# A fused Performer attention and MLP-Mixer kernel: one explicit order list, row-pair projections, and transposes moved to the DMA queue

## The chip, the cores and the metric

The kernel runs on one NeuronCore of a Trainium2 chip. The metric is the device time of one execution in microseconds (us); a case is timed by the median of several executions. The engines named below are TensorE (PE in the profile; PEld is its weight load), VectorE (DVE), ScalarE (ACT), GpSimd (POOL) and SyncE (SP, which here only issues DMAs). POOL issues the DMAs that convert float32 to float16.

## The reference

The inputs are `q`, `k`, `v` of shape (8 batches, 8 heads, 576 rows, 64), a feature matrix `omega` (128, 64), and four mixer weights. What is computed, cut to its core:

```python
def phi(x):                                   # positive random features
    proj = np.einsum('bhsd,md->bhsm', x, omega)
    sq = np.sum(x * x, axis=-1, keepdims=True) / 2.0
    h = proj - sq
    h = h - np.max(h, axis=-1, keepdims=True)
    return np.exp(h) / np.sqrt(m)
q_p, k_p = phi(q * scale), phi(k * scale)     # scale = 64 ** -0.25
kv  = np.einsum('bhsm,bhsd->bhmd', k_p, v)
z   = np.sum(k_p, axis=2)
num = np.einsum('bhsm,bhmd->bhsd', q_p, kv)
den = np.einsum('bhsm,bhm->bhs', q_p, z)[..., None] + 1e-06
x   = (num / den) as (8, 576, 512)

h  = np.maximum(x.transpose(0, 2, 1) @ w_tok1, 0.0) @ w_tok2   # 576 -> 256 -> 576
u  = x + h.transpose(0, 2, 1)
h2 = np.maximum(u @ w_ch1, 0.0) @ w_ch2                        # 512 -> 1536 -> 512
out = u + h2
```

## The kernel before

Each batch's 576 rows are split in 512 "main" rows and 64 "tail" rows. Two rows of 64 values stand side by side on the 128 partitions: partitions 0 to 63 of `qT` and `kT` hold one row of a pair, partitions 64 to 127 the other. For batches 0 and 1 this layout is made with TensorE transposes; for batches 2 to 7 `q` and `k` are first converted to float16 in DRAM (`cast_dram`) and then loaded by a transposing DMA (`load_T`).

The projection multiplies by `bd`, a 128 x 256 matrix that has `omega` transposed in two blocks on its diagonal and zeros elsewhere, so that one 128-deep contraction handles either row of the pair:

```python
def q_proj(b, hp, w):                # called twice per head pair: w = 0, 1
    ...
    ps = att_ps([P, 2, NP2], FP32, "q_ps")
    nc.tensor.matmul(
        ps, bd[:, w * M : (w + 1) * M], sb[:, 2 * hp : 2 * hp + 2, 0:NP2], start=True, stop=True
    )
    exp(live["qp", b, hp][:, w], ...)

def k_proj(b, hp, i):                # called twice per head pair: i = 0, 1
    ...
    ps = att_ps([P, 4, M], FP32, "k_ps")
    for e in range(2):
        nc.tensor.matmul(
            ps[:, 2 * e : 2 * e + 2, :],
            sb[:, 2 * hp + i, e * P : (e + 1) * P],
            bd, start=True, stop=True,
        )
    exp(live["kp", b, hp][:, i], ps)
```

`k_max` takes the maximum of the exponentials per row (two VectorE operations), its reciprocal, and multiplies `v` by it into `v_sc`. For batch 0 that multiplication runs on VectorE, for the others on GpSimd. Then `kv` (eight matmuls of 65 columns and two of 130) gives `kv_ps`, `num` gives `num_ps`, and `norm` divides into `xm`.

The mixer follows: `tok1` and `tok2` over the rows, then for each block of 128 rows a transpose of `u` on TensorE, which the channel layers need:

```python
def u_transpose(src, dst):
    ps = mix_ps([P, ND, P], FP16, "uT_ps")
    for db in range(ND):                                        # 4 transposes
        nc.tensor.transpose(ps[:, db, :], src[:, db * P : (db + 1) * P], ident16)
    nc.vector.tensor_copy(out=dst, in_=ps)

def ch1(c, cb):                      # 12 of these for each of 9 chunks c
    ps = mix_ps([P, SM], FP32, "h3_ps")
    for db in range(ND):             # 4 matmuls of 512 columns
        nc.tensor.matmul(ps, wc1[...], uT[:, db]..., start=(db == 0), stop=(db == ND - 1))
    nc.scalar.activation(out=live["r3", c][:, cb, :], in_=ps, func=AF.Relu)

def ch2(c, j):                       # 4 of these for each chunk
    ps = mix_ps([P, DM], FP32, "h2_ps")
    for cb in range(NCB):            # 12 matmuls of 512 columns
        nc.tensor.matmul(ps, live["r3", c][...], wc2[:, cb, :], ...)
    nc.vector.tensor_tensor(out=o, in0=u, in1=ps, op=ALU.add)
    nc.sync.dma_start(out=out[...], in_=o)
```

Chunk 8 collects the tails of all eight batches. [...]banks: three for `att_ps` (transposes and projections), two for `kn_ps` (`kv`, `num`), three for `mix_ps` (mixer).

[...]In this kernel every step has a place on a common time axis (numbers such as `u + o["kv"]`), and the steps are emitted sorted by place. At its start TensorE runs eight matmuls on zeros (`warm_ps`).

Of the kernel before, what the change touches and what calls it, by code (L numbers as in the profile page):

```python
# [9 lines left out]
FP32 = mybir.dt.float32  # L10
# [7 lines left out]
def kernel(  # L18
# [43 lines left out]
    def att_ps(shape, dt, name):  # L62
        return pspool.tile(shape, dt, name=name, tag="attps", bufs=3)
# [4 lines left out]
    def mix_ps(shape, dt, name):  # L68
        return pspool.tile(shape, dt, name=name, tag="mixps", bufs=3)
# [4 lines left out]
    live = {}  # L74

# [17 lines left out]
    def load_v(b):  # L93

        if b < 2:
            t = ldpool.tile([P, H, NJ, D], FP16, name="v_16", tag="v_16", bufs=2)
            live["v", b] = t
            nc.gpsimd.dma_start(
                out=t.rearrange("p h j d -> p h (j d)"),
                in_=v[b, :, 0:SM, :].rearrange("h (p j) d -> p h (j d)", j=NJ),  # L100
            )
            return
# [8 lines left out]
    def load_v_tail(b):  # L111
        t = ldpool.tile([P, 4, D], FP32, name="v_tail", tag="v_tail", bufs=2)
# [27 lines left out]
    def cast_qk(which):  # L140
        nc.vector.tensor_copy(out=live[which + "nat", 0][:, 0:2, :], in_=stage[which])
# [9 lines left out]
    warm = xt[0]  # L151
    nc.vector.memset(warm, 0.0)
    for b in range(2):
        new_nat(b)
# [5 lines left out]
    make_identity(nc, ident16)  # L160
    load_nat(0, 2, 4, "q")
    load_nat(0, 2, 4, "k")
    load_nat(0, 4, 8, "q")
    load_nat(0, 4, 8, "k")
    load_nat_tail(0, "k")
    load_nat_tail(0, "q")
    load_v(0)
# [5 lines left out]
    omega_nat = wpool.tile([P, 2 * D], FP16, name="omega_nat")  # L173
    nc.vector.tensor_copy(out=omega_nat[:, 0:D], in_=om_f)
    nc.vector.tensor_copy(out=omega_nat[:, D : 2 * D], in_=om_f)

    bd = wpool.tile([P, 2 * M], FP16, name="bd")
    nc.vector.memset(bd, 0.0)
# [11 lines left out]

    om_ps = att_ps([P, P], FP16, "om_ps")
# [3 lines left out]

    nc.vector.memset(w1t, 0.0)

    def clear_vz():
        for t in vz:
            nc.vector.memset(t, 0.0)  # L200

    def clear():
        nc.vector.memset(w2t, 0.0)
        nc.vector.memset(xt[1], 0.0)
        for t in q_pt:
            nc.vector.memset(t[:, 0:ST], 0.0)
            nc.vector.memset(t[:, SM + ST : SM + 2 * ST], 0.0)
# [10 lines left out]
    def permute_w2():  # L218
        for tb in range(NT):
            nc.vector.tensor_copy(  # L220
                out=w2m[:, tb], in_=w2raw[:, tb, 0:SM].rearrange("p (c j) -> p j c", j=NJ)
            )
            nc.vector.tensor_copy(out=w2t[:, tb, 0, 0:ST], in_=w2raw[:, tb, SM:S])
            nc.vector.tensor_copy(out=w2t[:, tb, 1, ST:P], in_=w2raw[:, tb, SM:S])
# [15 lines left out]
    steps = []  # L240

    def at(place, fn, *args):
        steps.append((place, len(steps), fn, args))


    def t_main(b, h0, n, which):

        if h0 == 0:
            live[which + "T", b] = ldpool.tile(
                [P, H, SP2], FP16, name=f"{which}T", tag=f"{which}T", bufs=2  # L250
            )
        ps = att_ps([P, n, 2, P], FP16, "t_ps")
# [5 lines left out]
        copy = nc.vector.tensor_copy if which == "q" else nc.scalar.copy  # L258
        copy(  # L259
# [4 lines left out]
    def t_tail(b, which):  # L264
# [4 lines left out]
        nc.vector.tensor_copy(out=live[which + "T", b][:, :, NP2:SP2], in_=ps)  # L269
# [32 lines left out]
    def k_tail_max(b, eng):  # L302
# [8 lines left out]
        for hh in range(4):  # L311
# [3 lines left out]
            eng.tensor_tensor(  # L315
# [6 lines left out]
    def q_proj(b, hp, w):  # L322
        sb = live["qT", b]
        if w == 0:
            live["qp", b, hp] = apool.tile([P, 2, 2, 2, P], FP16, name="q_p", tag="q_p", bufs=3)
        ps = att_ps([P, 2, NP2], FP32, "q_ps")
        nc.tensor.matmul(  # L327
            ps, bd[:, w * M : (w + 1) * M], sb[:, 2 * hp : 2 * hp + 2, 0:NP2], start=True, stop=True
        )
# [218 lines left out]
    for part in range(2):  # L548
        at(8 + O["kt"] + L["wc2"], load_wc2, part)
# [98 lines left out]
```

The softmax here doesn't subtract the row's maximum and nothing guards it: scores larger than these inputs give would overflow.

## Time and profile before

| what | value |
|---|---|
| time, median of 3 runs | 324.12 us (320.99 to 327.26) |
| span of the profiled execution | 318.9 us |
| VectorE busy | 173.8 us (55%) |
| ScalarE busy | 155.8 us (49%) |
| GpSimd busy | 71.6 us (22%) |
| DMA: packets on the queue of SP, on that of POOL, as a share of 16 engines' span | 32.4%, 26.2% |
| matmuls of `ch1` and `ch2` | 2 x 432, each 128 x 512 |
| projection matmuls | 64 of 128 x 512 (`q`), 128 of 128 x 256 (`k`) |
| TensorE transposes of `u` | 144 of 128 x 128 |

The span is read in slices: a row of 40 digits for each engine, where 9 means a slice of 8 us in which the engine was busy for 90% or more. A duration that the profile gives for a matmul is from its start to its modelled end; consecutive matmuls overlap, so the distance between starts, not the duration, is what one costs when the engine is full.

### The profile page before, as it was taken

The numbers are of one execution on the slowest core, as the hardware profiler recorded it, in microseconds if no ns is written. First come the engines' busy times: TensorE is split into PE (matmuls) and PEld (weight loads), VectorE is DVE, ScalarE is ACT, GpSimd is POOL, SyncE is SP. The second block draws the span as 40 slices with busy tenths as digits, with TensorE's granted clock in tenths as the row PEclk, the third lists the DMA queues.
The fourth block names the chain that finished last, engine by engine and source line by source line (L and its number), as shares of the span: only waits on it lengthen the run. The fifth ranks groups of instructions, "written<-read, shape, count | busy, mean of one in ns | idle before, by whom it ended". The sixth has DMA issues, their size and how long they took to land.

```text
span 318.9 us, 5525 instructions
## 1 busy us (share of the span) xinstructions
PE 299.3 (94%) x2137; PEld 159.1 (50%) x2137; DVE 173.8 (55%) x463; ACT 155.8 (49%) x299; POOL 71.6 (22%) x102
## 2 busy tenths in 40 slices
PE   5657889999999999999999999999999999999993
PEld 1435455555555555555555555555555444444441
DVE  3599996567455745674558456755385244002011
ACT  1557668633673367416842684358523610440610
POOL 9550535402141214121412131112311000000000
PEclk9598999999999999999999999999999999999998
DMA  7999999999990699059905991110011001002014
GB/s 150 195 195 211 192 244 213 196 238 205 153 256 35 128 173 244 25 123 175 259 3 128 158 238 54 68 66 2 1 67 68 0 27 74 33 2 102 30 39 92
DMA packets 59689, 38.75 MB, mean 121 GB/s; under 512 B 31120, under 2 KB 54544, under 8 KB 59280
## 3 DMA queue, kind: packets, MB, share of 16 engines
q1 hardware_dynamic: 48736, 24.16, 32.4%
q0 software_dynamic: 10656, 13.99, 26.2%
q8 instruction: 16, 0.26, 0.3%
q10 hardware_dynamic: 272, 0.26, 0.3%
q14 instruction: 9, 0.07, 0.1%
HBM read 35.88 MB, written 16.52 MB: 164 GB/s over the span
## 4 chain that ended last, share of the span: by engine, by line
PE 81%; DVE 10%; DMA 3%; POOL 3%; issue 1%; ACT 0%; POOLq 0%; DVEq 0%
PE h_ps L507 29%; PE h_ps L495 28%; PE ht_ps L457 4%; PE k_ps L339 3%; PE q_ps L327 3%; PE h_ps L441 3%; DMA v<-in_v_dram 3%; PE uT_ps L480 2%; PE num_ps L396 2%; PE kv_ps L372 2%; DVE xm L405 1%; PE kv_ps L377 1%; DVE km L355 1%; PE htt_ps L468 1%; POOL vz L315 1%
## 5 line engine op out<-in xcount | busy, mean ns | idle before, releaser
L507 PE MATMUL h_ps<-wc,r 128*128 128x512 f16 x432 | 98.1, 379 | 0.0
L502 ACT ACTIVATE r<-h_ps 128x512 f16<-128x512 f32 x108 | 64.8, 600 | 58.4 <-PE h_ps L495 56.2
L495 PE MATMUL h_ps<-uT,wc 128*128 128x512 f16 x384 | 93.0, 379 | 0.2 <-DVE uT L481 0.2
L507 PEld LDWEIGHTS <-r 128*128 128x128 f16 x432 | 41.0, 98 | 45.8
L495 PEld LDWEIGHTS <-wc 128*128 128x128 f16 x432 | 40.9, 98 | 41.3 <-issue 0.5
L360 POOL TENSOR_TENSOR v_sc<-v_nat,v_sc 128x512 f16<-128x512 f32 x24 | 25.4, 1058 | 130.5 <-DVE rc L404 91.4
L272 ACT ACTIVATE q_p<-q_ps 128x512 f16<-128x512 f32 x64 | 38.0, 599 | 33.1 <-PE q_ps L327 33.0
L516 DVE TENSOR_TENSOR o_sb<-um,h_ps 128x512 f32<-128x512 f16 x32 | 22.0, 688 | 48.0 <-PE h_ps L507 47.6
L272 ACT ACTIVATE k_p<-k_ps 128x512 f16<-128x512 f32 x64 | 37.8, 598 | 2.8 <-PE k_ps L339 1.5
L351 DVE TENSOR_TENSOR mx<-k_p 128x512 f16<-128x512 f16 x32 | 13.6, 425 | 37.0 <-ACT k_p L272 37.0
L405 DVE TENSOR_TENSOR xm<-num_ps,rc 128x256 f16<-128x256 f32 x64 | 27.1, 424 | 2.2
L385 ACT CAST kv_sb<-kv_ps 128x130 f16<-128x130 f32 x32 | 8.5, 266 | 39.1 <-PE kv_ps L377 39.0
L327 PE MATMUL q_ps<-qT,bd 128*128 128x512 f16 x64 | 24.9, 395 | 1.6 <-DVE qT L259 1.6
L339 PE MATMUL k_ps<-bd,kT 128*128 128x256 f16 x128 | 25.1, 282 | 0.9 <-ACT kT L259 0.9
L460 DVE TENSOR_TENSOR um<-xm,ht_ps 128x512 f16<-128x512 f16 x32 | 21.7, 683 | 4.0 <-PE ht_ps L457 3.9
L355 DVE TENSOR_REDUCE km<-mx 128x8 f16<-128x512 f16 x32 | 21.9, 686 | 1.1
L396 PEld LDWEIGHTS <-q_p 128*128 128x128 f16 x256 | 16.0, 99 | 10.5 <-issue 0.3
L315 POOL TENSOR_TENSOR vz<-v_tail,vz 32x256 f16<-32x256 f32 x28 | 17.3, 616 | 17.0 <-DVE vz L314 15.4
L457 PE MATMUL ht_ps<-r,w2m 128*128 128x512 f16 x64 | 19.0, 379 | 0.2
L396 PE MATMUL num_ps<-kv_sb,q_p 128*128 128x65 f16 x256 | 17.9, 195 | 0.1
L339 PEld LDWEIGHTS <-kT 128*128 128x128 f16 x128 | 12.1, 100 | 10.6 <-ACT kT L259 1.7
L441 PE MATMUL h_ps<-xm,w1m 128*128 128x512 f16 x64 | 16.4, 379 | 0.0
(93 smaller groups left out, 270.7 us busy)
## 6 DMA issues: line engine op xcount, KB each, us to landing
out_dram<-o_sb SPq DMA_DIRECT2D x32, 256.0 KB, 2.4
v_nat<-in_v_dram SPq DMA_DIRECT2D x12, 512.0 KB, 5.7
q<-in_q_dram POOLq DMA_DIRECT2D x6, 576.0 KB, 7.6
k<-in_k_dram POOLq DMA_DIRECT2D x6, 576.0 KB, 10.2
wc<-in_moe_w_ch_dram POOLq DMA_DIRECT2D x4, 768.0 KB, 14.9
v_tail<-in_v_dram SPq DMA_DIRECT2D x32, 32.0 KB, 4.7
v<-in_v_dram POOLq DMA_DIRECT2D x2, 512.0 KB, 8.6
out_dram<-o_sb SPq DMA_DIRECT2D x8, 128.0 KB, 2.3
```

What stands on the lines that cost most here:

```text
L272: nc.scalar.activation(out=out, in_=in_, func=AF.Exp, bias=0.0, scale=c_scale)
L327: nc.tensor.matmul(ps, bd[:, w * M : (w + 1) * M], sb[:, 2 * hp : 2 * hp + 2, 0:NP2], start=True, stop=True)
L339: nc.tensor.matmul(ps[:, 2 * e : 2 * e + 2, :], sb[:, 2 * hp + i, e * P : (e + 1) * P], bd, start=True, stop=True,)
L355: nc.vector.reduce_max(out=mx, in_=tmp, axis=AX.X)
L360: eng.tensor_tensor(out=vs[:, :, 0:D], in0=live["v", b][:, 2 * hp : 2 * hp + 2].rearrange("p h j d -> p (h j) d"), in1=vs[:, :, D : D + 1] ...
L396: nc.tensor.matmul(ps[:, j, :], live["qp", b, hp][:, j % 2, i, j // 2, :], sb, start=True, stop=True)
L405: nc.vector.tensor_tensor(out=live["x", b][:, :, h * D : (h + 1) * D], in0=ps[:, :, 0:D], in1=rc.unsqueeze(2).broadcast_to((P, NJ, D)), op ...
L441: nc.tensor.matmul(ps, w1m[:, j, tb * P : (tb + 1) * P], live["x", b][:, j, :], start=(j == 0), stop=False)
L457: nc.tensor.matmul(ps, w2m[:, tb, j, :], live["r1", b][:, tb, :], start=(tb == 0), stop=(tb == NT - 1))
L495: nc.tensor.matmul(ps, wc1[:, db, cb * P : (cb + 1) * P], uT[:, db].rearrange("p j c -> p (j c)"), start=(db == 0), stop=(db == ND - 1),)
L502: nc.scalar.activation(out=live["r3", c][:, cb, :], in_=ps, func=AF.Relu)
L507: nc.tensor.matmul(ps, live["r3", c][:, cb, j * P : (j + 1) * P], wc2[:, cb, :], start=(cb == 0), stop=(cb == NCB - 1),)
```

## The change

It does six things.

1. **One explicit list of steps.** The places on a time axis are gone; a text lists every step in its order ("proj 0 0; proj_exp 0 0 1; ..."), and the projection is split in two kinds of steps, the matmuls (`proj`) and each of the four exponentials (`proj_exp n`). In the list loads stand at other places than before: of batch 0, the `k` pieces, the `k` tail and the first half of `v` go ahead of the rest.
2. **Row-pair projections.** A matmul contracts over the 64 partitions of one row of the pair only. Matmuls on partitions 0 to 63 and 64 to 127 alternate and write to different banks. `att_ps` gets four banks, all of which one `proj` takes; `mix_ps` goes from three to two.
3. **The transposes of `u` for batches 2 to 7 and for the tails go over DRAM:** `u_write` stores the block, `load_uT` loads it by transposing DMAs on SP's queue. Batches 0 and 1 keep the TensorE transposes.
4. **Work moves between engines:** the `v` multiplications of batch 0 and the permutation of `w_tok2` to GpSimd, all zero fills to the start, and a table `SWAP` exchanges ScalarE and VectorE for single copies in batches 0 and 1.
5. **Zero matmuls in early gaps:** a table `HEAT` puts 27 matmuls of 128 x 512 on zeros ahead of named steps of batches 0 and 1.
6. `v_tail` gets one buffer in place of two.

The conversion of `q` and `k` in DRAM in large rows, which the change's description names too, is already in the kernel before: its function is the same in both, and only its places in the order differ.

The diff, cut to its core ("# ..." marks cuts):

```diff
     def att_ps(shape, dt, name):
-        return pspool.tile(shape, dt, name=name, tag="attps", bufs=3)
+        return pspool.tile(shape, dt, name=name, tag="attps", bufs=4)
# ...
     def mix_ps(shape, dt, name):
-        return pspool.tile(shape, dt, name=name, tag="mixps", bufs=3)
+        return pspool.tile(shape, dt, name=name, tag="mixps", bufs=2)
+    HEAT = {('kv', 0, 2): 1, ('kv', 1, 0): 3, ('kv', 1, 1): 2, ('num', 0, 0): 1, ('num', 0, 3): 1, ('num', 0, 4): 1, ('num', 0, 7): 1, ('proj', 0, 1): 1, ('proj', 1, 2): 4, ('t', 0, 0, 'q'): 3, ('t', 0, 4, 'k'): 2, ('t', 0, 6, 'k'): 4, ('t', 0, 6, 'q'): 3}
# ... (SWAP)
+    def heat(ps, *key):
+        for _ in range(HEAT.get(key, 0)):
+            nc.tensor.matmul(ps, warm[:, 0:P], warm, start=True, stop=True)
# ...
+    load_nat(0, 2, 4, "k")
     load_nat(0, 2, 4, "q")
-    load_nat(0, 2, 4, "k")
+    load_nat_tail(0, "k")
+    load_v(0, 0, 4)
+    load_nat(0, 4, 8, "k")
     load_nat(0, 4, 8, "q")
-    load_nat(0, 4, 8, "k")
-    load_nat_tail(0, "k")
     load_nat_tail(0, "q")
-    load_v(0)
+    load_v(0, 4, 8)
     load_v_tail(0)
# ...
-    def q_proj(b, hp, w):
# ...
-    def k_proj(b, hp, i):
# ...
+    def proj(b, hp):
+        qT, kT = live["qT", b], live["kT", b]
# ...
+        kps = [att_ps([P, 4, M], FP32, f"k_ps{w}") for w in range(2)]
+        qps = [att_ps([P, 2, NP2], FP32, f"q_ps{w}") for w in range(2)]
+        rows = [slice(w * D, (w + 1) * D) for w in range(2)]
+        om = [bd[rows[w], w * M : (w + 1) * M] for w in range(2)]
+        heat(kps[0], "proj", b, hp)
+        for t in range(4):
+            for w in range(2):
+                nc.tensor.matmul(
+                    kps[w][:, t, :],
+                    kT[rows[w], 2 * hp + t // 2, (t % 2) * P : (t % 2 + 1) * P],
+                    om[w],
+                    start=True,
+                    stop=True,
+                )
+        for w in range(2):
+            nc.tensor.matmul(
+                qps[w], om[w], qT[rows[w], 2 * hp : 2 * hp + 2, 0:NP2], start=True, stop=True
+            )
+        live["pps", b, hp] = kps + qps
# ...
+    def u_write(b, j):
+        if j == 0:
+            live["u16", b] = dpool.tile([SM, DM], FP16, name="u16", tag="u16")
+        src = live["u", b][:, j, :] if b < B else ut[j]
+        nc.sync.dma_start(out=live["u16", b][j * P : (j + 1) * P, :], in_=src)
+
+    def load_uT(b):
# ...
+        for db in range(ND):
+            nc.sync.dma_start_transpose(
+                out=dst[:, db].rearrange("p j c -> p (j c)"),
+                in_=live["u16", b][:, db * P : (db + 1) * P],
+            )
# ...
-    for _, _, fn, args in sorted(steps, key=lambda s: s[:2]):
-        fn(*args)
+    order = """
+        load_nat 1 0 4 k; load_nat 1 0 4 q; cast_qk k; load_nat 1 4 8 k; cast_qk q; t_main 0 0 2 q;
+        load_nat_tail 1 k; t_main 0 2 2 q; t_main 0 0 2 k; t_main 0 2 2 k; t_tail 0 k; proj 0 0; proj_exp 0 0
# ... (73 more lines)
+    """
# ...
+    for step in order.split(";"):
+        name, *args = step.split()
+        steps[name](*(int(a) if a.isdigit() else a for a in args))
```

A piece of the new list from the middle, with `ch1` steps beside exponentials and other TensorE steps:

```
... ch2 0 0; kv 2 2; ch1 1 0; ch1 1 1; ch1 1 5; proj_exp 2 3 1; ch1 1 7; num 2 2 1; k_max 2 3;
proj_exp 2 3 3; ch1 1 3; num 2 2 0; q_tail 3; ch1 1 2; norm 2 2 1; proj 3 0; proj_exp 3 0 2; ...
```

## The prediction, written before the changed kernel was run

> **What bounds the kernel now.** I read the page's busy shares and slices first, then a table of stretches, the instructions in order of time in a middle stretch, and last the chain of work that ended last. The slices:
>
> ```profile
> PE 299.3 (94%) x2137; PEld 159.1 (50%) x2137; DVE 173.8 (55%) x463; ACT 155.8 (49%) x299; POOL 71.6 (22%) x102
> PE   5657889999999999999999999999999999999993
> DVE  3599996567455745674558456755385244002011
> PEclk9598999999999999999999999999999999999998
> DMA  7999999999990699059905991110011001002014
> ```
>
> TensorE is full from the seventh slice on, but not in the first six (48 us); there VectorE shows 9 in four slices, and DMA is full for twelve. The TensorE clock falls in the second and fourth slice. So there are two stages with two limits. The table of stretches has the same in microseconds:
>
> ```profile
> core 0: us, PE busy (x) PEld busy (x) DVE busy (x) ACT busy (x) POOL busy (x), PEclk, DMA share, GB/s
> 10.00:20.00 10.00, 5.72 (x58) 3.61 (x57) 7.18 (x26) 5.40 (x11) 5.57 (x8) 0.71 1.39 198
> 20.00:30.00 10.00, 7.49 (x84) 5.18 (x85) 9.55 (x29) 7.07 (x14) 2.07 (x4) 0.83 1.37 222
> 30.00:40.00 10.00, 7.79 (x96) 4.88 (x96) 9.29 (x31) 6.39 (x13) 4.32 (x6) 1.00 1.08 177
> 40.00:50.00 10.00, 8.80 (x89) 5.29 (x87) 9.43 (x26) 6.78 (x14) 2.72 (x5) 1.00 1.18 250
> 140.00:180.00 40.00, 40.00 (x303) 21.93 (x301) 24.55 (x66) 20.39 (x41) 9.41 (x13) 1.00 0.72 149
> ```
>
> From 20 to 50 us VectorE is busy 28.3 of 30 us; from 140 to 180 us TensorE 40.0 of 40. A busy TensorE may still be stretched, so I took the cost of each kind of matmul from the distances of starts in the middle:
>
> ```profile
> 109.67 0.38 PE L327 MATMUL q_ps<-qT,bd 128*128 128x512 f16 x1
> 109.89 0.38 PE L339 MATMUL k_ps<-bd,kT 128*128 128x256 f16 x2
> 110.10 0.39 PE L480 MATMUL uT_ps<-ident,um 128*128 128x128 f16 x4
> 110.33 0.38 PE L278 MATMUL qt_ps<-qT,bd 128*128 128x256 f16 x2
> 110.54 0.29 PE L396 MATMUL num_ps<-kv_sb,q_p 128*128 128x65 f16 x4
> ```
>
> A 512-column matmul costs 0.216 us (twelve of `ch2` stand in the chain with 2.59 us), a 256-column one 0.108 (109.89 to 110.10 for two), a transpose 0.056 (0.23 for four), a 65-column one about 0.03 (0.12 to 0.13 for four). For two batches: 248 of 512 columns make 53.5 us, 40 of 256 make 4.3, 144 of 65 make 4.3, 16 of 130 about 0.9, 36 transposes 2.0; in all 65.0 us. The chain shows the `tok2_tail` matmuls of consecutive pairs of batches at 73.09, 138.60 and 204.10 us, 65.5 apart. So the middle is TensorE issuing with hardly a hole: only TensorE work taken away can shorten it. The same sum over the whole program is about 286 us. The span is 318.9; the last matmuls end near 314, which leaves some 5 us of output at the end. The rest, 28 us, is lost in the first 48 us, before the first `ch1` at 48.08.
>
> What holds that first stage, from the chain in order of time:
>
> ```profile
> 5.75 9.02 DMA v<-in_v_dram
> 14.86 0.69 DVE v_sc L360
> ...
> 19.99 0.43 DVE mx L351
> 20.45 0.70 DVE km L355
> 21.42 0.69 DVE v_sc L360
> 22.24 0.42 DVE xm L405
> 22.79 0.42 DVE xm L405
> 23.91 0.70 DVE km L355
> ```
>
> First the load of `v`, issued seventh on its queue, then VectorE one operation after another up to 47 us.
>
> **What the Trainium skill says.** "TensorEngine Tiling (Array Packing)", section Theoretical Speedup: a contraction of at most 64 can use two tiles of 64 rows at once, up to twice as fast. No matmul before does so; no run here shows it yet. The same page, Key Properties: changing the tiling mode drains TensorE. The trace before has 32-row transposes (`tt_ps`) only beside DMA waits, so it gives no cost of a switch. "TensorE: Matmul & The Clock Gate", section Part 1, The HAM clock gate: the default clock is half and sustained activity releases it. The trace agrees: the mean clock is 0.71 and 0.83 in the 10 to 30 us stretches with their holes, and the eight warm-up matmuls take 631 ns in the mean against 379 later. "DMA: Bandwidth & Descriptors", section Issuing engines are not separate DMA queues: transfers from all issuers share 16 engines; so the new transposing loads compete with the casts. Here these engines are full up to 96 us and mostly idle after 200.
>
> **Part by part.**
>
> *Row-pair projections.* `q`: 64 matmuls x 0.216 = 13.8 us; as 32 pairs side by side 6.9, so 6.9 less. `k`: 128 x 0.108 = 13.8 us; after it 256 matmuls of 128 columns, which as 128 pairs at the 0.056 of a transpose (also a weight load and 128 columns) cost 7.2, so 6.6 less. If pairs did not overlap, `k` would cost 256 x 0.056 = 14.3 and nothing would be gained. Against this stand 64 changes of mode (into and out of 32 `proj` steps). A full drain would be the part of a matmul's duration beyond its start distance, 0.379 - 0.216 = 0.163 us; 64 of these are 10.4 us. I take half, 5. Net: 13.5 - 5 = 8.5 us less, all in a stage in which TensorE sets the end, except for two batches of eight.
>
> *Transposes of `u`.* 28 of 36 blocks go: 112 x 0.056 = 6.3 us of TensorE, all in the full stage. VectorE loses 28 copies of 0.416 us, which is beside the path. The new DMA work is 28 writes of 128 KB and 28 transposing loads of 128 KB. The loads of `q`/`k` of 576 KB land in 6.9 and 6.2 us in the median, so a quarter of one should take some 2 to 4 us; a store to `out` lands in 2.4. In the list several `ch1` and `ch2` steps (0.86 and 2.59 us each) stand between `u_write` and the use, for chunk 7 at the end about 26 us of them. I expect these transfers hidden.
>
> *The first stage.* Off VectorE between 6 and 48 us go three multiplications by `v` (3 x 0.69, a fourth stays; one of batch 1 comes to it), four of the tails (4 x 0.42), zero fills (some 2.0: two of 0.54, two of 0.27 and small ones) and the `w_tok2` permutation (1.5): about 6.5 us net. Adding up what VectorE must do in the new order from the bias copies at 5.8 us to the first `ch1` with the durations of the page gives 30 us, so it cannot start before 36 us, against 48.08. `v` in halves, asked for fourth, should arrive about 4 us earlier than 14.8. GpSimd's 1.06 us per multiplication, its waits for DMA slots in between, and loads of batch 2 that still come through full DMA engines take some of this back. I take 8 us.
>
> *Zero matmuls.* 27 x 0.216 = 5.8 us, double at half clock, in a stage with 28 us of holes: nearly free, and the clock stays up. I charge 1 us.
>
> *Two mixer banks.* A `ch1` group started at 48.08 has its ReLU at 49.14 for 0.60; with 0.05 of signalling the bank is free 1.71 us after the group's start. Two groups take 1.73. So it just fits if ScalarE comes at once; an exponential (0.60) ahead of the ReLU makes TensorE wait some 0.3 us, unless a `num`, `kv` or `proj` stands between, as the list often has it. I charge 2 us, for some seven unhidden waits.
>
> Sum: -8.5 - 6.3 - 8 + 1 + 2 = -19.8. The list is plainly tuned as a whole (single copies are swapped between engines), which makes me lean a little further: -23, hence **301 us**.
>
> **Rivals.**
> (a) *The drain eats the pairs.* For it: the page's sentence, and that weight loads (98 ns each) double in number for `k`. Against: it needs the full 0.163 us at every switch. Then -19.8 becomes about -14: 310 us.
> (b) *Two mixer banks turn ScalarE into the bound.* For it: the fit of 1.71 in 1.73 us, and 128 exponentials to place. If half of them cost 0.3 us, 19 us come back: 318 us. Against: ScalarE is busy only 20.4 of 40 us in the middle.
> (c) *The DMA path becomes the wait.* For it: DMA full to 96 us, SP's queue in order, a store that waits for `um` holding up the transposes of `q` behind it. If each of seven chunks waits 2 us: about 315 us.
> (d) *The first stage gains more:* its 28 us of loss shrink to 12, and pairs are switched freely: 290 us.
>
> **Range and chances.** From (d) to (b) with most weight between: 289 to 314. To stay within 2% (317.6 or more) nearly all gains must be given back; to be slower, a stall in every batch must appear. Faster 0.87, same 0.09, slower 0.04.
>
> **What would show it.** Pairs: two `k_ps` matmuls of 128 columns starting within a few ns of each other, and a `proj` of about 0.45 us from first start to the next step's start. Drain: a hole of 0.1 to 0.2 us in starts before and after each `proj`. Transposes: 32 `uT_ps` matmuls in place of 144 and no wait of `ch1` for a DMA. First stage: first `ch1` near 40 us, clock 1.0 after 10 us. Banks: waits of `ch1` for the ReLU, a few tenths each. I am wrong if the middle's distance between pairs of batches stays above 63 us, or if the first `ch1` is not earlier than 45 us.

## The result, and the profile after

| | before | changed |
|---|---|---|
| time, median of 4 runs each | 322.56 us (320.71 to 327.26) | 308.23 us (307.22 to 308.76) |
| ratio, with its 95% interval | | 0.958 (0.951 to 0.964) |
| span of the profiled execution | 318.9 us | 305.4 us |

The change takes off 14.3 us by the medians and 13.5 us by the profiled spans (12.5 us against the 320.6 to 320.9 us that the kernel before had in the later series of runs). The prediction, 301 us with a range from 289 to 314, had the direction and the range right; it asked for 23 us, 9 more than came.

The page of the changed kernel, its busy shares and its slices (slices of 7.6 us now):

```profile
PE 290.9 (95%) x2180; PEld 143.4 (47%) x2180; DVE 161.4 (53%) x418; ACT 157.4 (52%) x305; POOL 79.3 (26%) x115
PE   7788899999999999999999999999999999999993
DVE  5588984764587677456553468447643420021021
PEclk9999999999999999999999999999999999999998
DMA  8999999999979989969899997341241243333021
```

The clock row has no dip left. The PE row starts with 7 and 8 where before had 5 and 6, but that counts zero matmuls as work. The table of stretches of the changed kernel still has two stages:

```profile
core 0: us, PE busy (x) PEld busy (x) DVE busy (x) ACT busy (x) POOL busy (x), PEclk, DMA share, GB/s
10.00:20.00 10.00, 8.60 (x91) 4.28 (x89) 7.45 (x21) 7.87 (x17) 7.79 (x11) 1.00 1.43 186
20.00:30.00 10.00, 8.00 (x119) 5.25 (x119) 8.21 (x26) 8.88 (x17) 7.00 (x13) 1.00 1.08 164
30.00:40.00 10.00, 8.64 (x88) 4.32 (x86) 9.52 (x24) 4.95 (x11) 6.44 (x10) 1.00 0.87 157
40.00:50.00 10.00, 9.67 (x89) 5.15 (x88) 6.23 (x18) 6.21 (x13) 0.00 (x0) 1.00 1.15 177
140.00:180.00 40.00, 40.00 (x283) 19.42 (x282) 19.16 (x49) 20.66 (x41) 8.04 (x11) 1.00 0.99 195
```

VectorE still holds the larger part of the first stage: it is busy 9.52 of 10 us from 30 to 40, and the chain of work that ended last runs mostly through it from 20.6 to 39.4 us. Before that the chain runs through the load of `k` up to 11.1 us and then through ScalarE and TensorE. The middle is still TensorE (40.00 of 40). In the middle one projection looks like this, in the instructions in order of time of the changed kernel:

```profile
181.78 0.59 PE L475 MATMUL ht_ps<-r,w2m 128*128 128x512 f16 x2
182.31 0.40 PE L338 MATMUL k_ps<-bd,kT 64*128 64x128 f16 x8
182.54 0.38 PE L346 MATMUL q_ps<-qT,bd 64*128 64x512 f16 x2
182.85 0.60 PE L475 MATMUL ht_ps<-r,w2m 128*128 128x512 f16 x2
```

Eight `k` matmuls of 128 columns start within 0.23 us (182.31 to 182.54), and the two `q` matmuls of 512 columns cost what one does: the pairs run side by side. The hole ahead of them is 182.31 - 181.78 - 2 x 0.216 = 0.10 us, the hole behind 182.85 - 182.54 - 0.216 = 0.09 us. So entering and leaving the 64-row form costs 0.19 us per projection.

To see where the 13.5 us lie I did the prediction's sum of start distances again for every kernel: so many matmuls of each kind, each at its own distance (0.216 us for 512 columns, 0.1085 for 256, 0.058 for 130, 0.056 for 128, 0.0312 for 65; 0.0288 for a `k` matmul of a pair, 0.108 for a `q` matmul of a pair), split at the first `ch1`. "Idle" is all the rest of the time up to the last matmul's end: waits, half-clock time and mode changes. The distances are rounded, so an entry is uncertain by a few tenths.

| us | first `ch1` | work before it | of it zeros | idle before it | work after it | idle after it | end of matmuls |
|---|---|---|---|---|---|---|---|
| before | 48.08 | 24.0 | 0 | 24.1 | 264.4 | 1.4 | 313.9 |
| changed | 42.60 | 25.3 | 5.8 | 17.3 | 249.2 | 8.6 | 300.4 |

Matmul work falls by 13.9 us: real work by 19.7, which within the table's uncertainty are the 13.5 of the pairs and the 6.3 of the transposes as predicted, against 5.8 us of added zero matmuls. Idle time is nearly the same in sum, 25.5 and 25.9 us: 6.8 us less before the first `ch1`, 7.2 us more after it.

### The profile page after: what moved, and what is told of

Its sections match the earlier page's. It is cut to its first block, busy times and chain, and to the rows that moved or that the text cites. A ratio compares the mean times of both kernels' runs of the same rounds, so it can differ in the third digit from the quotient of the medians.

```text
span 305.4 us, 5665 instructions
## 1 busy us (share of the span) xinstructions
PE 290.9 (95%) x2180; PEld 143.4 (47%) x2180; DVE 161.4 (53%) x418; ACT 157.4 (52%) x305; POOL 79.3 (26%) x115
## 4 chain that ended last, share of the span: by engine, by line
PE 80%; DVE 11%; ACT 2%; POOL 2%; DMA 2%; issue 1%; DVEq 0%; POOLq 0%
PE h_ps L542 29%; PE h_ps L530 29%; PE ht_ps L475 4%; PE h_ps L459 3%; PE num_ps L414 2%; PE k_ps L338 2%; PE kv_ps L388 2%; DMA k_nat<-in_k_dram 2%; DVE km L366 2%; DVE xm L423 2%; PE q_ps L346 2%; DVE mx L362 2%; PE htt_ps L486 1%; PE kv_ps L393 1%; PE heat_ps L166 1%
## 5 line engine op out<-in xcount | busy, mean ns | idle before, releaser
L537 ACT ACTIVATE r<-h_ps 128x512 f16<-128x512 f32 x108 | 64.7, 599 | 71.3 <-PE h_ps L530 71.2
L542 PE MATMUL h_ps<-wc,r 128*128 128x512 f16 x432 | 97.0, 379 | 0.0
L530 PE MATMUL h_ps<-uT,wc 128*128 128x512 f16 x384 | 90.7, 379 | 0.1
L530 PEld LDWEIGHTS <-wc 128*128 128x128 f16 x432 | 40.1, 98 | 43.6 <-issue 2.0
L275 ACT ACTIVATE k_p<-k_ps 128x512 f16<-128x512 f32 x64 | 37.0, 605 | 12.5 <-PE k_ps L338 10.0
L478 DVE TENSOR_TENSOR um<-xm,ht_ps 128x512 f16<-128x512 f16 x32 | 21.5, 684 | 15.3 <-PE ht_ps L475 14.6
L318 POOL TENSOR_TENSOR vz<-v_tail,vz 32x256 f16<-32x256 f32 x32 | 20.3, 635 | 20.2 <-DVE vz L317 18.4
L475 PE MATMUL ht_ps<-r,w2m 128*128 128x512 f16 x64 | 18.9, 380 | 2.0 <-DVE r L468 1.0
L414 PEld LDWEIGHTS <-q_p 128*128 128x128 f16 x256 | 14.3, 98 | 13.2 <-issue 2.5
L414 PE MATMUL num_ps<-kv_sb,q_p 128*128 128x65 f16 x256 | 17.0, 194 | 1.4 <-DVE kv_sb L401 1.2
L362 DVE TENSOR_TENSOR mx<-k_p 128x512 f16<-128x512 f16 x32 | 15.4, 482 | 4.5 <-ACT k_p L275 4.2
L422 DVE RECIPROCAL rc<-num_ps 128x4 f32<-128x4 f32 x64 | 10.8, 169 | 10.5 <-PE num_ps L414 10.2
L401 ACT CAST kv_sb<-kv_ps 128x130 f16<-128x130 f32 x30 | 8.2, 272 | 13.9 <-PE kv_ps L393 13.8
L346 PE MATMUL q_ps<-qT,bd 64*128 64x512 f16 x64 | 14.4, 375 | 0.6 <-ACT q_p L275 0.3
L388 PEld LDWEIGHTS <-k_p 128*128 128x128 f16 x256 | 11.4, 98 | 6.5 <-issue 1.7
```

Source lines behind the costliest of these rows:

```text
L275: nc.scalar.activation(out=out, in_=in_, func=AF.Exp, bias=0.0, scale=c_scale)
L362: nc.vector.tensor_tensor(out=tmp, in0=kp[:, :, 0 : M // 2], in1=kp[:, :, M // 2 : M], op=ALU.max)
L414: nc.tensor.matmul(ps[:, j, :], live["qp", b, hp][:, j % 2, i, j // 2, :], sb, start=True, stop=True)
L475: nc.tensor.matmul(ps, w2m[:, tb, j, :], live["r1", b][:, tb, :], start=(tb == 0), stop=(tb == NT - 1))
L530: nc.tensor.matmul(ps, wc1[:, db, cb * P : (cb + 1) * P], uT[:, db].rearrange("p j c -> p (j c)"), start=(db == 0), stop=(db == ND - 1),)
L542: nc.tensor.matmul(ps, live["r3", c][:, cb, j * P : (j + 1) * P], wc2[:, cb, :], start=(cb == 0), stop=(cb == NCB - 1),)
```

## The experiments

The changed kernel was run beside the kernel before in one series, the experiments beside the kernel before in later ones, where that had a median of 320.6 to 320.9 us. So an experiment stands against the changed kernel through two ratios, and a difference of less than about 2 us says little. "More than the changed kernel" below is against its 308.2 us. The table of work and idle time, for all of them (in runs 2 and 7, what the pairs cost above the distances given stands under idle time):

| us, from one profile each | ratio to before (95%) | median | first `ch1` | idle before it | work after it | idle after it |
|---|---|---|---|---|---|---|
| changed | 0.958 (0.951 to 0.964) | 308.2 | 42.60 | 17.3 | 249.2 | 8.6 |
| 1 no zero matmuls | 0.975 (0.971 to 0.979) | 313.0 | 44.09 | 24.6 | 249.2 | 12.7 |
| 2 one half, then the other | 0.969 (0.965 to 0.973) | 310.9 | 42.96 | 17.7 | 249.2 | 10.3 |
| 3 projections 128 deep | 0.975 (0.972 to 0.978) | 312.7 | 43.25 | 14.6 | 259.3 | 2.4 |
| 4 `u` transposed on TensorE | 1.027 (1.023 to 1.031) | 329.1 | 42.69 | 17.4 | 255.5 | 23.8 |
| 5 work back on VectorE | none | 318.5 | 45.38 | 20.1 | 249.2 | 23.3 |
| 6 old first loads | 0.973 (0.970 to 0.976) | 312.0 | 46.31 | 21.0 | 249.2 | 10.0 |
| 7 both series on one half | 0.991 (0.988 to 0.994) | 317.9 | 45.96 | 20.7 | 249.2 | 17.3 |
| 8 as 4, later in the list | 1.015 (1.008 to 1.022) | 324.3 | 43.23 | 17.9 | 255.5 | 18.8 |
| 9 more banks for the mixer, one load earlier | 0.973 (0.972 to 0.975) | 312.4 | 44.23 | 18.9 | 249.2 | 11.0 |
| 10 no zero matmuls, one load earlier | 0.980 (0.977 to 0.983) | 314.0 | 43.99 | 24.5 | 249.2 | 13.4 |
| 11 as 9, 15 zero matmuls | 0.972 (0.970 to 0.974) | 311.2 | 43.61 | 20.9 | 249.2 | 13.8 |
| 12 before, with `u` over DRAM | 1.148 (1.147 to 1.150) | 368.0 | 47.48 | 23.5 | 258.2 | 55.4 |

The first `ch1` itself varies from one profile to the next: runs 4, 8 and 9 have the changed kernel's list up to that point, and it comes at 42.69, 43.23 and 44.23 us in them.

### 1. Without the zero matmuls

```diff
-    HEAT = {('kv', 0, 2): 1, ('kv', 1, 0): 3, ... ('t', 0, 6, 'q'): 3}
+    HEAT = {}
```

> The changed kernel without its 27 zero matmuls (the 8 at the start stay). Theory A: they keep the TensorE clock at 1.0 in the first 48 us; without them the clock falls to 0.75 to 0.85 between 10 and 30 us and the time is 2 to 5 us longer. Rival B: row pairs and the denser order keep the clock up by themselves, and the zero matmuls only stand in the way (the chain of the changed kernel runs through 1.02 + 0.75 + 0.57 us of them); without them the clock stays at 1.0 and the time is 1 to 3 us shorter.

It took 313.0 us, 4.8 more. Before the first `ch1` the loss is small: idle time plus zeros were 17.3 + 5.8 = 23.1 us with them, and the idle time is 24.6 without. The matmuls of this run are stretched between 7 and 16 us (eight `k` matmuls at 12.32 us take 0.61 us, where the changed kernel has 0.40, though the clock column of this run reads 1.00 there), but the first `ch1` comes only 1.5 us later, within the spread just named. Run 10, also without zeros, has a granted clock of 0.50 from 10 to 20 us and its first `ch1` at 43.99. Nor do the zeros secure the clock: runs 7 and 9 have all 27 and show 0.66 and 0.77 there. The larger part, 4.1 us, comes later, though all zero matmuls stand before. The instructions in order of time of this run show the main piece:

```profile
115.67 0.81 PE L530 MATMUL h_ps<-uT,wc 128*128 128x512 f16 x3
119.17 0.58 PE L530 MATMUL h_ps<-uT,wc 128*128 128x512 f16 x1 [2.69 <-DMA uT<-u]
119.55 0.42 PE L414 MATMUL num_ps<-kv_sb,q_p 128*128 128x65 f16 x4
```

`ch1` of chunk 2 waits 2.69 us for its transposing loads. The queue of SP issues these four loads, in the changed kernel and then in this run (start, time that issuing took):

```profile
103.92 5.13 SPq L518 DMA_TRANSPOSE uT<-u  x4
105.40 8.10 SPq L518 DMA_TRANSPOSE uT<-u  x4
```

In the changed kernel they are just in time: the fourth lands at 115.0 us, 7.2 us after its issue, and the fourth `ch1` matmul starts 0.17 us late for it. In this run the loads and their first use (115.67 in place of 114.18) both come 1.5 us later, so being late does not by itself make a wait. The fourth load does: it is issued 2.1 us later, holds the queue for 3.65 us in place of 1.26, and lands 9.3 us after its issue. At 109.07 us, 0.8 us ahead of it, GpSimd issues the conversion of the next `q` to float16; in the changed kernel that conversion is issued at 107.92, 0.13 us behind the fourth load. That the two transfers are in each other's way fits this and is not shown. After the wait the matmuls are stretched (0.58 us for one of 0.38): the clock has dropped. Experiments 9 to 11 take this up.

### 2. All matmuls of one row half, then all of the other

```diff
-        for t in range(4):
-            for w in range(2):
+        for w in range(2):
+            for t in range(4):
# and the q matmul of half w directly behind its four k matmuls
```

> The changed kernel with the same 64-deep projection matmuls, but all those on partitions 0 to 63 first and then all those on 64 to 127. Theory: two matmuls on different halves of the rows run side by side; without alternation a projection's matmuls take 8 x 0.056 + 2 x 0.216 = 0.88 us in place of 0.45, 0.43 us more, which for 24 projections in the full stage is 10.4 us and with part of the early eight 11 to 14 us more. Rival: a 64-deep matmul is cheaper by itself and the order of issue does not matter; the time is the same within 2 us.

It took 310.9 us, 2.7 more, where the theory asked for 11 to 14. The program has the order `k k k k q` for half 0 and then the same for half 1. The trace has another; in order of time:

```profile
184.02 0.41 PE L338 MATMUL k_ps<-bd,kT 64*128 64x128 f16 x7
184.25 0.38 PE L345 MATMUL q_ps<-qT,bd 64*128 64x512 f16 x1
184.27 0.22 PE L338 MATMUL k_ps<-bd,kT 64*128 64x128 f16 x1
184.32 0.38 PE L345 MATMUL q_ps<-qT,bd 64*128 64x512 f16 x1
184.63 0.60 PE L474 MATMUL ht_ps<-r,w2m 128*128 128x512 f16 x2
```

Seven `k` matmuls start before the first `q` matmul, although three of them stand behind it in the program. The half 1 series runs beside half 0 one matmul late, and a projection is 0.61 us long in place of 0.54. The Trainium skill says, in "TensorE: Matmul & The Clock Gate", section Part 3: Packing small matmuls, that "MATMULs are pc-monotone in start AND end", so without reordering. The trace differs for starts of matmuls in different row halves, and the trace decides. So this run can't tell whether pairs run side by side; that needed a run in which both series meet in one half, number 7.

### 3. The old 128-deep projections in the new kernel

```diff
-        for t in range(4):
-            for w in range(2):
+        for i in range(2):
+            for e in range(2):
                 nc.tensor.matmul(
-                    kps[w][:, t, :], kT[rows[w], ...], om[w], ...
+                    kps[i][:, 2 * e : 2 * e + 2, :], kT[:, 2 * hp + i, e * P : (e + 1) * P], bd, ...
# q likewise, from all 128 partitions; k_max and kv follow the other layout of k_ps
```

> The changed kernel with the projection matmuls of the kernel before (128 deep against the zero-filled block matrix: 4 of 256 columns, 2 of 512), everything else as changed. Theory: a projection costs 0.87 us of TensorE and no change of mode, against 0.45 plus two holes of 0.095 us = 0.64; so 0.23 x 32 = 7.4 us more, 6 to 8 us because some of the early eight hide. Rival 1: the changes of mode eat the gain, 0 to 2 us. Rival 2: the pairs bring their full 13.5 us.

It took 312.7 us, 4.5 more, where the theory asked for 6 to 8. The pairs save 13.5 us of streaming, and 9 of these go: idle time is 25.9 us with pairs and 17.0 without. Of the 8.9 us, 32 x 0.19 = 6.1 are mode changes. Another 1.6 lie after the first `ch1`, at least half of it in waits that a projection of 0.86 us covers in part and one of 0.45 covers less; two of them in the changed kernel, in order of time:

```profile
80.07 0.40 PE L388 MATMUL kv_ps<-v_sc,k_p 128*128 128x65 f16 x8 [0.27 <-POOL v_sc L374]
...
89.94 0.59 PE L475 MATMUL ht_ps<-r,w2m 128*128 128x512 f16 x2 [0.52 <-DVE o_sb L551]
```

Each stands behind a projection or one step after it; the first waits for the multiplication by `v`, the second for a mixer bank (a `mix_ps` buffer). From start to start they cost 0.33 and 0.68 us, and with the longer projections 0.11 and 0.29. The last 1.2 us lie before the first `ch1`, which hardly moves: 43.25 us with 3.4 us more of matmul work in front of it, against 42.60, which is within its spread. TensorE alone doesn't set that time, so the pairs bring far less than 3.4 us there.

### 4. `u` transposed on TensorE again

```diff
-        u_write 2 0; tok2 2 2; u_write 2 3; ...   load_uT 2
+        tokT 2 0; tok2 2 2; tokT 2 3; ...         # no load_uT
```

> The changed kernel with all transposes of u on TensorE again: each u_write becomes a transpose at its place in the list, and the loads are left out. Theory: 112 transposes x 0.056 = 6.3 us more of TensorE, and a further 1 to 5 us where a transpose directly follows its sum: 7 to 11 us more in all. Rival: the transfers over DRAM cost as much as they saved by waits and by crowding the DMA engines; then the time is the same within 2 us.

It took 329.1 us, 20.8 more, and is slower than the kernel before. The transposes themselves are 6.3 us of the work after the first `ch1`; 15.2 us are new idle time. I suspected the place: `tokT` stands directly behind the `tok2` whose result it transposes, so TensorE waits for VectorE's sum. Number 8 tests that.

### 8. The same, with the transposes where `load_uT` stood

```diff
-        num 3 2 0; load_uT 2; kv 3 3; norm 3 2 0; proj 4 0; num 3 3 1; ...
+        num 3 2 0; tokT 2 0; kv 3 3; tokT 2 1; norm 3 2 0; proj 4 0; tokT 2 2; num 3 3 1; tokT 2 3; ...
```

> The changed kernel with all transposes of u on TensorE, but each chunk's four at the place where the changed kernel loads them back, one matmul step apart, and not directly after their sums. With them at the place of the stores the time was 22 us above the changed kernel: 6.3 us of matmuls and 16 us of holes. Theory: the holes came from waits for the sum directly ahead and for the two mixer banks; placed later, the waits for the sum go and the time is 7 to 13 us above the changed kernel, of which 6.3 are the transposes and the rest waits for a bank. Rival: the transposes cost this much wherever they stand; again about 20 us above.

It took 324.3 us, 16.1 more; 6.3 us of work and 10.2 of idle time after the first `ch1` remain. So the early place cost some 5 us and is not the main cause. In order of time, near the end:

```profile
253.88 0.39 PE L498 MATMUL uT_ps<-ident,ut 128*128 128x128 f16 x4
254.73 1.02 PE L533 MATMUL h_ps<-uT,wc 128*128 128x512 f16 x4 [0.46 <-ACT r L540]
255.59 0.39 PE L498 MATMUL uT_ps<-ident,ut 128*128 128x128 f16 x4
256.44 1.02 PE L533 MATMUL h_ps<-uT,wc 128*128 128x512 f16 x4 [0.46 <-ACT r L540]
```

A `uT_ps` group of 0.22 us stands between two `ch1`. The `ch1` behind it needs the bank of the `ch1` before it, whose ReLU on ScalarE is not done, and 0.63 us pass (254.73 - 253.88 - 0.22) in which no matmul starts. Eleven of the 28 groups have a hole of 0.62 to 0.72 us behind them, 7.0 us together; with the smaller holes beside the others that is all of the new idle time. So with two mixer banks a short mixer step between two `ch1` costs such a wait. The kernel before has three banks and all 144 transposes, and its idle time after the first `ch1` is 1.4 us. So moving the transposes off TensorE and giving `mix_ps` two banks belong together: without the first, the second costs more than the 6.3 us that the transposes stream. A changed kernel with three mixer banks was not run.

### 7. Both series on the same half

```diff
+        rows, om = [rows[0], rows[0]], [om[0], om[0]]
```

Both series read partitions 0 to 63; the projections of the rows on partitions 64 to 127 are left out, and those of the others are done twice. Number and shape of all instructions are unchanged.

> The changed kernel in which both series of a projection's matmuls read partitions 0 to 63; it leaves out the rows on partitions 64 to 127 (their results are copies of the other half's), all counts and sizes stay. Theory: side by side run only matmuls on different halves; without a second half a projection takes 8 x 0.056 + 2 x 0.216 = 0.88 us and the two holes of the mode change, 0.43 us more; 10 to 13 us more in all. That issuing one half after the other cost only 3.4 us then means that TensorE takes matmuls out of its queue ahead of their turn. Rival: 64-deep matmuls are cheap by themselves; within 2 us.

It took 317.9 us, 9.6 more. A projection in order of time:

```profile
180.55 0.62 PE L339 MATMUL k_ps<-bd,kT 64*128 64x128 f16 x8
181.00 0.59 PE L347 MATMUL q_ps<-qT,bd 64*128 64x512 f16 x2
181.53 2.76 PE L531 MATMUL h_ps<-uT,wc 128*128 128x512 f16 x12
```

Eight `k` matmuls now need 0.45 us and the two `q` 0.43, twice the 0.23 and 0.216 of the changed kernel. So the two halves of the array do work at the same time there, and that is worth about 10 us here.

### 6. The old order of the first loads

```diff
-    load_nat(0, 2, 4, "k")
     load_nat(0, 2, 4, "q")
-    load_nat_tail(0, "k"); load_v(0, 0, 4); load_nat(0, 4, 8, "k")
+    load_nat(0, 2, 4, "k")
     load_nat(0, 4, 8, "q")
+    load_nat(0, 4, 8, "k"); load_nat_tail(0, "k")
     load_nat_tail(0, "q")
-    load_v(0, 4, 8)
+    load_v(0, 0, 8)
```

> The changed kernel with the first loads of batch 0 in the order of the kernel before (q, k, q, k, k tail, q tail, v in one piece). Theory: v and the k tail asked for earlier let the first kv start earlier; with the old order v lands near 14.8 us in place of about 11, so the first stage ends 2 to 4 us later and the time is 2 to 4 us longer. Rival: the k pieces and not v were on the chain, and the 16 engines are shared anyway; within 1 us.

It took 312.0 us, 3.8 more. The first `ch1` comes 3.7 us later, and idle time before it is 3.7 us longer. In the table of stretches of this run:

```profile
10.00:20.00 10.00, 7.83 (x69) 3.84 (x70) 4.78 (x15) 6.11 (x12) 4.64 (x7) 0.67 1.15 153
```

VectorE is busy 4.78 of 10 us, against 7.45, and the clock is 0.67. Which of the moved loads is missed, TensorE shows in this run:

```profile
11.49 0.39 PE L270 MATMUL tt_ps<-ident,natt 32*128 32x32 f16 x8 [2.83 <-DMA natt<-in_k_dram]
```

It waits for the tail of `k`, which the changed kernel transposes at 8.22 us; the first exponential comes 3.3 us later (12.46 in place of 9.18), and about this shift stays. So the new order of the first loads is worth 3.7 us before the first `ch1`, and it is passed on to the end in full. What the earlier `v` adds was not tested alone.

### 5. The moved work back on VectorE

```diff
-        (nc.vector if ("v", b, hp) in SWAP else nc.gpsimd).tensor_tensor(   # v_sc
+        (nc.vector if b == 0 else nc.gpsimd).tensor_tensor(
# the tails of batch 0 and the w_tok2 permutation go from gpsimd to vector likewise
```

> The changed kernel with batch 0's multiplications by v (three more of 0.69 us, four tails of 0.42) and the w_tok2 permutation (1.5 us) back on VectorE: 5.2 us more work there before the first ch1. Theory: VectorE holds the first stage, which in the changed kernel it fills to 7.5, 8.2 and 9.5 of 10 us between 10 and 40 us; the first ch1 comes 2 to 5 us later than 42.6 and the time is 2 to 5 us longer. Rival: GpSimd's slower multiplication (1.06 us) and its DMA work held the chain as much; then the time is within 1 us of the changed kernel or shorter.

Its four times spread from 312.5 to 324.3 us, so no ratio is given and the size stays open; the fastest is 4.3 us above the changed kernel. The profile is of the 324.3 one. In order of time, TensorE and then GpSimd in the same run:

```profile
49.67 0.28 PE L393 MATMUL kv_ps<-vz,k_pt 128*128 128x130 f16 x2
58.05 2.31 PE L530 MATMUL h_ps<-uT,wc 128*128 128x512 f16 x5 [8.11 <-DMA wc<-in_moe_w_ch_dram]
```

```profile
37.82 1.06 POOL L374 TENSOR_TENSOR v_sc<-v,v_sc 128x512 f16<-128x512 f16 x1 [2.27 <-DVE v_sc L370]
40.27 1.06 POOL L374 TENSOR_TENSOR v_sc<-v,v_sc 128x512 f16<-128x512 f16 x1 [1.39 <-DVE v_sc L370]
41.27 0.84 POOL L235 DMA_DIRECT2D wc<-in_moe_w_ch_dram  x1
```

The second half of `wc1` is issued from GpSimd, in order behind multiplications that wait for VectorE: 41.27 us here, 38.61 in the changed kernel. In this execution `ch1` waits 8.11 us for it. The later issue is only 2.7 us of that; the transfer itself lands 16.7 us after its issue, 8.1 us in the changed kernel, and why is not shown. That the same happens in the faster executions was not seen.

### 9 to 11. Slack for the mixer's banks and for chunk 2

After the last exponential the `att_ps` banks lie unused, and the changed kernel waits for a mixer bank at 242 and 247 us. And chunk 2's loads looked as if they wanted to be issued earlier. Number 9 does both, number 10 the earlier load without zero matmuls, number 11 is number 9 with 15 of 27 zero matmuls:

```diff
     def mix_ps(shape, dt, name):
+        if "last exp" in live:
+            turn["n"] += 1
+            if turn["n"] % 2:
+                return att_ps(shape, dt, name)
# the list, in all three:
-        u_write 2 2; ch1 1 8; proj_exp 3 3 1; num 3 1 0; ... load_v_all 4; ... num 3 2 0; load_uT 2; kv 3 3;
+        u_write 2 2; ch1 1 8; proj_exp 3 3 1; load_uT 2; num 3 1 0; ... load_v_all 4; ... num 3 2 0; kv 3 3;
```

> The changed kernel with two mends. After the last exponential every second mixer step takes one of the four att banks, which are free by then; and chunk 2's transposing loads are issued right after its last store, ahead of the next batch's v and the stores to out. Theory: two mixer banks leave a hole of 0.42 us at each short step when no attention work stands beside it (two at the end, at 241.6 and 246.4 us), and the loads of chunk 2 land just in time; 1 to 2 us less than the changed kernel. Rival: both are within the spread; no difference, within 0.7 us.

> The changed kernel without the 27 zero matmuls and with chunk 2's transposing loads issued right after its last store. Without the zero matmuls alone the time was 5.5 us more, of which the trace puts 1.5 us before the first ch1 (44.06 in place of 42.60) and about 4 us to a wait of chunk 2 for its loads at 116 us and the half clock after it. Theory: that wait is a question of where the loads stand; with them earlier it goes and the time is 1 to 2.5 us above the changed kernel. Rival: the zero matmuls are worth 5 us by the clock itself; again 4 to 6 us above.

> As e9, with 15 of the 27 zero matmuls: those that lie on the chain of the changed kernel (before the transposes of heads 6 and 7, kv of batch 1, proj 1 2) are cut or halved. Theory: the clock stays at 1.0 with half of them and the chain loses 1 to 2 us; 1 to 2 us less than e9. Rival: the clock falls in one of the early stretches; 0 to 4 us more than e9.

They took 312.4, 314.0 and 311.2 us. Numbers 9 and 10 missed; number 11 is 1.2 us below number 9 by the medians and 0.5 by the ratios, too little to tell. In number 9 the two holes at the end are gone, some 0.8 us. But there is a new one, and all three have it; here number 9, TensorE in order of time:

```profile
115.08 0.38 PE L352 MATMUL q_ps<-qT,bd 64*128 64x512 f16 x2
118.88 0.40 PE L396 MATMUL kv_ps<-v_sc,k_p 128*128 128x65 f16 x8 [3.42 <-POOL v_sc L382]
```

and the queue of SP in the same run (the second number is the time that issuing took):

```profile
98.38 1.86 SPq L519 DMA_DIRECT2D u<-um  x4
101.95 5.56 SPq L526 DMA_TRANSPOSE uT<-u  x4
107.56 1.21 SPq L121 DMA_DIRECT2D v_nat<-in_v_dram  x2
108.81 2.76 SPq L130 DMA_DIRECT2D v_tail<-in_v_dram  x4
```

The transposing loads wait for the last store of `u`, occupy the queue to 107.5 us, and `v` of batch 4, which the changed kernel issues at 97.89, comes 9.7 us later (2.4 of them because this run is that late at its first store of `u`). `kv` then waits 3.42 us for the multiplication by `v`. So at this place the list has little room: behind `v`, a slower fourth load stops `ch1`; ahead of `v`, the loads stop `kv`. Another 1.6 us of number 9 lie before the first `ch1`, where nothing was changed; the clock is 0.77 there from 10 to 20 us, as said, and what lowers it is not shown.

They also put a bound on the zero matmuls. Numbers 9 and 11 share everything but 12 zero matmuls, and their ratios agree (0.973 and 0.972). Number 10 against number 9 has no zero matmuls and not the extra banks, and is 1.6 us slower, 0.8 of which are the banks'. So their own worth is about 1 us, no more than the noise; the 4.8 of number 1 is mostly chunk 2's wait and the lower clock behind it (0.97 and 0.94 in the stretches from 100 to 140 us).

### 12. `u` over DRAM in the kernel before

```diff
+        mv = tokT if b < 2 else u_write
-        items += [(1, tokT, b, 0), (2, tok2, b, 2), (1, tokT, b, 1), (2, tok2, b, 3)]
+        items += [(1, mv, b, 0), (2, tok2, b, 2), (1, mv, b, 1), (2, tok2, b, 3)]
# load_uT behind the last u_write; the channel steps of chunks 1 to 8 start 0.9 of a place later
```

> The kernel before with one part alone: the transposes of u for batches 2 to 7 and for the tails over DRAM, and the channel steps from chunk 1 on placed 0.9 of a head pair's turn later so that the loads can land; three mixer banks, the old projections and the old first stage stay. Theory: only TensorE's 112 transposes go, 6.3 us; 5 to 7 us less than before. That undoing them in the changed kernel cost 18 to 22 us is then due to its two mixer banks and its order, not to the transposes themselves. Rival: the transposes cost as much with three banks; 15 us or more less than before. A third: chunks wait for their loads and nothing is gained.

It took 368.0 us, 47 more than the kernel before. The waits of this run, TensorE's part:

```profile
PE h_ps L511 <- DMA uT<-u: 37.6, 13, 10.6
```

`ch1` waits 13 times for `uT`, 37.6 us in all and up to 10.6 at once, and the clock falls to 0.83 to 0.93 from 100 to 220 us. Taking 6.3 us of transposes off TensorE loses seven times as much here. The loads come late because the stores ahead of them do. In the waits of SP's queue from 98 to 125 us of this run stands

```profile
SPq L88 <- DMA q<-in_q_dram: 10.5, 1, 10.5
```

The queue holds until 109.1 us for the conversion of the next `q`, whose transposing load it has to issue first. Three of chunk 2's four stores stand behind that load and others and are issued at 119.25 us and later, though the last of their sums on VectorE starts at 106.32. So this run does not say what the DRAM path is worth in the kernel before; it says that its stores and loads need a place on the queue that nothing else holds up.

## Why the prediction was right in direction and 9 us off in size

| term | predicted | measured | from |
|---|---|---|---|
| pairs, streaming | -13.5 | -13.5 | 0.23 and 0.216 us for the two series; work table; run 7 |
| mode changes | +5 | +6.1 | 0.19 x 32 |
| transposes of `u` | -6.3 | -6.3 | 112 fewer |
| first stage, with zeros | -8 + 1 = -7 | -2.5 | idle 24.1 to 17.3, plus 5.8 of zeros, less 8 x 0.19 counted above |
| two mixer banks | +2 | +2.6, of it 1.5 for banks | idle 1.4 to 8.6, less 24 x 0.19; banks: waits at 89.9, 242.2 and 247.1 us |
| sum | -19.8 | -13.6 | TensorE's end: 313.9 to 300.4, -13.5 |

**Pairs.** Right, with the sign it named: starts side by side, a hole of 0.1 before and after. It allowed half a full drain, 0.08 us per change; 0.095 was measured. A projection takes 0.54 us from start to the next step's start where it named 0.45, which leaves out the hole behind it. Taken back alone (run 3), though, the pairs are worth 4.5 us and not the 8.5 of the prediction's net: what they free is in part idle time, before the first `ch1` and in waits that longer projections had covered. The sign of the middle, a distance between pairs of batches below 63 us, can't be read: the new list does not keep it even, and the `tok2_tail` matmuls start 56.7, 69.8 and 49.1 us apart.

**Transposes.** Right as work taken away: 32 in place of 144, and in the changed kernel one hole of `ch1` in front of a DMA, of 0.17 us. What it didn't see is that undoing it costs 16 to 21 us: with two banks a short mixer step brings a wait of some 0.6 us. Rival (b), two banks turning ScalarE into the bound, is not what the changed kernel shows (its ReLUs wait for TensorE, 71.2 us in all); without the DRAM path (runs 4 and 8) the two banks do become the wait.

**The first stage is the step that failed:** "I take 8 us", and "I charge 1 us" for the zero matmuls. The first `ch1` came at 42.60 us, between the "near 40" and the 45 that it named as signs of right and wrong. But an earlier first `ch1` is not a gain of the same size. At 42.60 us the changed kernel had done 19.5 us of real matmul work, the one before 24.0 at 48.08. Of the difference 3.4 us are the pairs of the eight projections that lie there, already counted in the 13.5, and 1.1 is work that comes later in the new list. Take these from 5.5 and 1.0 remains, 2.5 without the mode changes. The sum thus counted the early pairs twice, once as streaming and once as an earlier `ch1`; run 3 shows that they hardly move that time by themselves. And the zero matmuls fill 5.8 of the 6.8 us of idle time that went away. Some of them stand in the chain itself; the chain of the changed kernel has

```profile
13.26 0.50 ACT k_p L275
13.80 1.02 PE heat_ps L166 x4
15.05 0.38 PE k_ps L338 x8
...
17.12 0.29 PE tt_ps L271 x8
17.41 0.75 PE heat_ps L166 x3
18.39 0.36 PE kv_ps L388 x8
```

with 1.02 and 0.75 us of zeros between one step and the next. The prediction's 30 us of VectorE work from 5.8 us on were right (29.3 are measured up to the first `ch1`), but it took VectorE to be kept busy from there: it stands idle 7.5 us, 4.6 of them ahead of 20.6 us, while the chain runs through a load, ScalarE and TensorE. The order of the first loads was worth 3.8 us (run 6).

**The lean of 3 us** for a list tuned as a whole had no working, and the sum of the measured terms leaves nothing for it. Without it the prediction would have been 304. The list as a whole, the table `SWAP` and the single `v_tail` buffer were not tested alone.

**Rival (c)**, DMA paths becoming the wait, shows in the changed kernel as no more than the 0.17 us at 115 us but stands close behind it: runs 1, 5, 9 and 12 all fall into it, each by a load that came later than something needed it. **Rival (d)** failed with the first stage.

## What to carry to other kernels

Count a gain by the work that TensorE has done by a point, not by how early the point comes: a stage that another engine holds turns removed matmuls into idle time, and an event in it comes earlier when its work is put off as well as when it is done faster. When two banks feed a step's evacuation, look at every step shorter than that evacuation, and see whether it can leave the engine altogether. In a list tuned by hand, a load moved earlier on an in-order queue delays the loads behind it, so ask which of those has no slack before asking what the moved one gains.

## What the runs showed of the hardware that was not expected

- Matmuls of the other row half start ahead of their turn in the program (run 2), and issuing one half wholly ahead of the other costs 2.7 us in 32 projections, where a strict order would have cost about 10 (run 7).
- Entering and leaving the 64-row form beside 128-row matmuls costs 0.10 and 0.09 us. The Trainium skill, "TensorEngine Tiling (Array Packing)", section Key Properties, states that the change drains TensorE and gives no figure; here it is 0.6 of the 0.163 us that I had taken for a full drain.
- Four transposing loads of 128 KB each hold SP's issuing queue for 5.0 to 8.0 us in the changed kernel, and their data land 2.4 to 11.0 us after issue (3.4 in the median), while a plain store of 128 KB lands in 2.1. The prediction's 2 to 4 us was the median, not the range that a list has to allow for.
